# A planned single-core kernel that mixes a recurrent attention with a full attention: new ranks for its list scheduler, smaller filler pieces, and a new way to issue the start-up loads

## The chip, the cores and the metric

The kernel runs on one core of one Trainium2 chip. The metric is device time in microseconds (us) of one execution, as the median of several runs. Five engines work side by side: TensorE (PE, its weight loads shown as PEld), VectorE (DVE), ScalarE (ACT), GpSimd (POOL) and SyncE (SP). Each runs its own instructions strictly in the order of the program and waits on semaphores. Loads and stores are issued from SP's and ACT's instruction streams.

## The reference, cut to what matters

Two attentions read the same input `x` (2048 rows of 576) and their outputs are mixed by a gate per row.

```python
# A: 64 segments of 32 rows, 32 heads of 128; 8 memory rows go from segment to segment
for s in range(n_seg):
    h = concat([mem, xs])                      # 40 rows
    q, k, v = h @ Wq, h @ Wk, h @ Wv           # 576 -> 32 x 128 each
    p = softmax(mask(q k^T * scale))
    o = (p v) @ Wo
    mem = o[:8]; outs.append(o[8:])            # mem feeds the next segment
# B: full attention over 2048 rows, 32 heads of 18
qkv = x @ wqkv;  b = softmax(q k^T * scale) v @ wo
return g * a + (1 - g) * b                     # g = sigmoid(sum(x * gate_w))
```

A is a chain of 64 dependent segments. B has no such order and serves as filler work beside it.

## The kernel before, in words

**The planner.** The kernel first builds some thousands of `Op` objects with `add(name, engines, duration, fn, deps, prio, mode, take, give, tail)`. `Plan.run` is a list scheduler. It simulates the engines with the written durations, a cost of 0.1 us when TensorE changes its tiling mode (`SWITCH`), a delay from one engine to the next (`DRAIN`) and, for loads and stores, a landing time (`tail`). At each step `Plan.choose` takes, among the operations that could start within 0.03 us of the first, the one of smallest `prio` (plus 0.4 if it changes TensorE's mode). Operations with `prio` under 1 can hold back a longer one. The result is only an order: the instructions are emitted in it, and on the chip each waits for its real data. A dependency that stands only in `deps` and not in the data makes no instruction wait. Buffers are counted as tokens (`plan.tokens_of`): three PSUM banks `pb`, one `sb` of four banks for B's scores, one `ob` for B's output.

**Start-up.** `x_tile` loads 16 tiles of `x` (alternately from SP and ACT), has POOL duplicate a narrow part (`xd`), transposes on TensorE into `xT`, and evacuates with DVE and ACT. ACT's stream also issues `wqkv` (`load_wb`) and then, by `load_w`, the three A weights `wv`, `wq`, `wk`: 12 DMAs and 4.7 MB each. `project_qk` and `project_v` compute B's q, k and v and store them to DRAM (tiles `stg`, `vt`), from where `load_k`, `load_v`, `load_q` fetch them by head. `last_unit` computes q, k, v of A's last 8 rows of each segment (PE tiles `pv`, stored from `vl`): 24 units for the first 16 segments before the recurrence, and 72 later as filler, in pieces of 0.57 us or 1.1 us. `opening` marks the point where B's start-up buffers are given back; `wo` (4.7 MB) is loaded then.

**Recurrence.** For segment `s`: load of the segment's 24 rows into `ht` (`ld_h`, three DMAs on SP), six projections (`project`: Q0, K0, Q1, K1, V0, V1; PE tile `pvv`), evacuation to `tm`, `turn` (PE tile `pt`), copy to `qk`, scores `psh`, exp, mask `mn`, sums `sm` (tile `pss`), reciprocal `rq`, broadcast `bc` (tile `prb`), normalising into `et`, `pso` (needs V: `put_v`, eight DMAs `v_sb<-tm` on SP), copy to `ot`, output product in 8 pieces (`out_pieces`, tile `acc`), `obf` and `bd`, and `fold` (tile `pw`), which makes the next memory and writes it into the next `ht`. Every four segments `lo0`/`lo1` do the output product of the last rows. `st_a` stores each segment's output with four DMAs.

**B as filler.** 512 visits `sb` (four score matmuls), `ex` (exp on ACT, 2048 columns) and `ob` (four value matmuls). Visit `i` may not be planned before a segment's Q0: `ahead` visits are free, the others are spread evenly over the 64 segments; `sb` has `prio` 0.

**End.** B's output product (`po`), times the gate, plus A's rows reloaded from DRAM and multiplied on POOL (`ga`).

## Time and profile before

| | us |
|---|---|
| median of 3 runs (1756.57 to 1763.96) | 1757.65 |
| the profiled execution | 1751.69 |
| its span, first to last instruction | 1749.9 |
| TensorE busy in it | 1471.1 |
| ACT busy | 1099.5 |
| DVE busy | 715.0 |
| POOL busy | 133.2 |
| mean granted TensorE clock | 0.945 of full speed |

The span leaves 1.8 us of the execution's own time around it. Busy times add up over stages that differ: start-up, the 64 segments, the end. A stage has to be read by itself.

### The profile page before, as it was taken

Reading aid. Unit: us, or ns where it says so; the run is one execution under the profiler, and the core shown is the slowest. Engines: PE = TensorE matmul, PEld = TensorE weight load, DVE = VectorE, ACT = ScalarE, POOL = GpSimd, SP = SyncE. Lnnn points to the kernel's source line nnn. Section 1 sums busy time; section 2 is a strip of 40 time slices with the busy share of each in tenths; the row PEclk is TensorE's granted clock in tenths of the full one; section 3 lists DMA queues with packets and bytes.
Section 4 is the critical chain, followed back from the end, with each engine's and each line's share of the span. In section 5 each row is a group of like instructions: output and inputs, shape, how many; then the busy total and the mean of one; then the engine's idle time right before and its main releaser. Section 6 shows DMA issues by size and latency. Waiting matters only on the chain. (4 is left out here: it accounts for less than half of the span.)

```text
span 1749.9 us, 68709 instructions
## 1 busy us (share of the span) xinstructions
PE 1471.1 (84%) x30560; PEld 844.8 (48%) x30582; DVE 715.0 (41%) x1523; ACT 1099.5 (63%) x872; POOL 133.2 (8%) x295
## 2 busy tenths in 40 slices
PE   2387788988898988889889889888989888888886
PEld 2243544555555544455555444555555444444444
DVE  2143234444344444443434443444444444434444
ACT  1024678888776666666656666665767666667672
POOL 4000000000000000000000000000000000000024
PEclk9989889999999999999999989999999898899998
DMA  7746322111221111111222111112222111111131
GB/s 259 261 126 183 58 41 54 47 29 36 59 40 33 39 48 49 39 33 33 49 44 42 34 37 39 47 35 41 38 48 59 30 30 32 40 24 33 27 118 66
DMA packets 285727, 104.21 MB, mean 60 GB/s; under 512 B 222263, under 2 KB 281911, under 8 KB 283895
## 3 DMA queue, kind: packets, MB, share of 16 engines
q1 hardware_dynamic: 281079, 82.50, 20.2%
q10 hardware_dynamic: 4352, 17.33, 2.7%
q8 instruction: 239, 3.92, 0.9%
q14 instruction: 57, 0.47, 0.1%
HBM read 52.09 MB, written 30.86 MB: 47 GB/s over the span
## 5 line engine op out<-in xcount | busy, mean ns | idle before, releaser
L680 ACT ACTIVATE etb<-sb 128x2048 bf16<-128x2048 f32 x512 | 961.4, 1878 | 432.0 <-PE sb L671 400.2
L333 DVE CAST tm<-pvv 128x512 bf16<-128x512 f32 x312 | 214.9, 689 | 235.8 <-PE pvv L980 198.1
L980 PEld LDWEIGHTS <-ht 128*32 128x32 bf16 x7680 | 199.2, 97 | 203.7 <-issue 21.4
L671 PE MATMUL sb<-qch,kch 32*128 32x512 bf16 x2048 | 210.0, 398 | 57.1 <-ACT etb L680 55.9
L689 PE MATMUL ob<-etb,vch 128*32 128x512 bf16 x2048 | 213.4, 407 | 7.2 <-ACT etb L680 7.2
L908 PE MATMUL acc<-wo,ot 128*32 128x144 bf16 x8192 | 182.5, 253 | 10.0 <-DVE ot L333 8.1
L908 PEld LDWEIGHTS <-ot 128*32 128x32 bf16 x8192 | 165.0, 111 | 29.8 <-DVE ot L333 15.8
L980 PE MATMUL pvv<-wq_m,ht 128*32 128x512 bf16 x2048 | 138.6, 388 | 14.5 <-DVE ht L1175 13.8
L671 PEld LDWEIGHTS <-kch 32*128 32x128 bf16 x2048 | 62.8, 91 | 179.0 <-issue 157.1
L1047 DVE COPY qk<-pt 128x1024 bf16<-128x1024 bf16 x128 | 88.1, 688 | 143.3 <-PE pt L1039 142.6
L333 DVE CAST ot<-pso 128x320 bf16<-128x320 f32 x176 | 82.7, 484 | 142.6 <-PE pso L1124 141.3
L980 PE MATMUL pvv<-wk_m,ht 128*32 128x512 bf16 x2048 | 137.4, 385 | 0.0
L980 PE MATMUL pvv<-wv_m,ht 128*32 128x512 bf16 x2048 | 134.1, 379 | 0.0
L950 POOL COPY qk<-xl 128x256 bf16<-128x256 bf16 x128 | 53.2, 418 | 1051.9 <-PE psh L1060 852.4
L689 PEld LDWEIGHTS <-vch 128*32 128x32 bf16 x2048 | 55.0, 94 | 117.5 <-issue 115.3
L1124 PE MATMUL pso<-et,v_sb 64*128 64x40 bf16 x2048 | 62.8, 183 | 51.2 <-DMA v_sb<-tm 36.4
L1039 PE MATMUL pt<-ident,tm 128*128 128x128 bf16 x1024 | 78.6, 219 | 9.9 <-DVE obf L1204 5.4
L331 ACT CAST ot<-pso 128x320 bf16<-128x320 f32 x80 | 34.0, 426 | 83.4 <-PE pso L1124 82.8
L1124 PEld LDWEIGHTS <-v_sb 64*128 64x128 bf16 x2048 | 43.4, 96 | 80.9 <-DMA v_sb<-tm 47.6
L1039 PEld LDWEIGHTS <-tm 128*128 128x128 bf16 x1024 | 61.4, 97 | 42.4 <-issue 40.5
L1113 DVE TENSOR_TENSOR et<-et,prb 128x320 bf16<-128x320 bf16 x128 | 59.1, 485 | 24.0 <-PE prb L1103 21.3
L1153 DVE CAST obf<-acc 128x144 bf16<-128x144 f32 x64 | 19.7, 307 | 120.6 <-PE acc L908 88.3
(117 smaller groups left out, 1452.6 us busy)
## 6 DMA issues: line engine op xcount, KB each, us to landing
v_sb<-tm SPq DMA_DIRECT2D x512, 32.0 KB
qkd<-vl SPq DMA_DIRECT2D x64, 128.0 KB
xl<-qkd SPq DMA_DIRECT2D x64, 128.0 KB
wo<-in_A_Wo_dram SPq DMA_DIRECT2D x4, 1152.0 KB
wv_m<-in_A_Wv_dram ACTq DMA_DIRECT2D x4, 1024.0 KB
vgd<-vt SPq DMA_DIRECT2D x32, 128.0 KB
wq_m<-in_A_Wq_dram ACTq DMA_DIRECT2D x4, 1024.0 KB
wk_m<-in_A_Wk_dram ACTq DMA_DIRECT2D x4, 1024.0 KB
```

The lines of the kernel that those rows point to most:

```text
L331: nc.scalar.copy(out=out_of(), in_=in_of())
L333: nc.vector.tensor_copy(out=out_of(), in_=in_of())
L671: nc.tensor.matmul(sb[:, j, :], lhsT=kc[r, o:o + P], rhs=qt_[r, :], start=True, stop=True, tile_position=(32 * j, 0),)
L680: nc.scalar.activation(out=etb[:, :, :], in_=box["sb", gq, kb][:, :, :], func=ACT.Exp, scale=scale_b)
L689: nc.tensor.matmul(ob[32 * j:32 * j + 32, :], lhsT=vc[:, o + 32 * j:o + 32 * j + 32], rhs=etb[:, j, :], start=(kb == 0), stop=(kb == NKB - ...
L908: nc.tensor.matmul(acc[32 * j:32 * j + 32, :], lhsT=o[:, slot, t0:t0 + CT], rhs=wo[:, h, RW * j:RW * j + RW], start=(first and s_ == 0), s ...
L950: nc.gpsimd.tensor_copy(out=opened["qk"][:, f, :, 0:16 * L].rearrange("p a (h t) -> p a h t", t=L)[:, :, :, CT:L], in_=box["xlt", s][:, :, ...
L980: nc.tensor.matmul(pv[32 * j:32 * j + 32, :], lhsT=ht[:, cc, :], rhs=rw, start=(c == 0), stop=(c == NF), tile_position=(0, 32 * j), skip_g ...
L1039: nc.tensor.transpose(out=pt[:, a, :, i, :], in_=tm[:, i * Dh:(i + 1) * Dh], identity=ident[:, :])
L1047: nc.vector.tensor_copy(out=opened["qk"][:, hf, :, 0:16 * L].rearrange("p a (h t) -> p a h t", t=L)[:, :, :, 0:CT], in_=box["pt", s, hf][: ...
L1113: nc.vector.tensor_tensor(out=et[:, :], in0=et[:, :], in1=box["prb", s, hf][:, :], op=ALU.mult)
L1124: nc.tensor.matmul(ps[jj][:, r * L:(r + 1) * L], lhsT=v_sb[rr, hf * 1024 + r * Dh:hf * 1024 + (r + 1) * Dh], rhs=et[rr, r * L:(r + 1) * L] ...
```

## The change

The fixed priorities become entries of a table `RANK`, and some constants of the scheduler too (the cost of a mode switch 0.4 to 0.358, the window 0.03 to 0.016, the hold-back rules). Visits: `ahead` 60 to 23, `behind` 6 to 0. A unit of filler (`last_unit`) is cut into four or five pieces, and may be planned only after `psh0` of its segment instead of after Q0; `lo0`/`lo1` of a group are planned in the next segment, after its `psh0`. The A weights are issued by SP in 12 chunks of three DMAs, each planned after the last but one has landed; `wqkv` by SP too, `gw` later. The memsets of POOL become planned operations, `xd` goes from POOL to DVE. More buffers: `xn` 6 to 8, `stg` 4 to 6, `vt` 3 to 6, `vl` 2 to 3. The segment's rows come from one load of three DMAs per four segments (`ld_x` into `xg`) and three POOL copies per segment (`put_x`); `st_a` stores four segments with four DMAs. SP's planned time of `put_v` goes from 1.8 to 2.4 us.

```diff
+RANK = {
+    "switch": 0.358, "near": 0.016, "early": 0.142, "wait": 0.207, "Q0": 1.286, "K0": 1.258, "Q1": 1.601,
+    "K1": 1.792, "V0": 1.857, "V1": 1.908, "t0": 0.05, "t1": 0.05, "ph0": 1.897, "ph1": 1.655, "sm0": 1.072,
+    "sm1": 1.075, "bc0": 1.274, "bc1": 1.098, "po0": 0.49, "po1": 0.786, "op0": 1.401, "op1": 0.286,
+    "fo": 0.05, "lo0": 2.219, "lo1": 2.052, "la": 1.802, "ob": 1.25, "eQ": 3.281, "eK": 2.028, "eV": 1.472,
+    "co": 0.984, "le": 5.423, "xp": 0.119, "mn": 0.05, "fin": 3.122, "la_gate": 1, "lo_gate": 1, "ahead": 23,
+    "behind": 0, "tail": 0.059,
+}
...
-    for t_ in kring + qring + [wo7]:
-        nc.gpsimd.memset(t_[:], 0.0)
...
+    z_wb = zero("zwb", wb[TL:P, NF, :], 1.6, 0.05)
...
-    plan.tokens_of("xn", 6)
+    plan.tokens_of("xn", 8)
...
-    plan.tokens_of("stg", 4)
-    plan.tokens_of("vt", 3)
+    plan.tokens_of("stg", 6)
...
-        du = add(f"xd{n}", "POOL", 0.35, dup, [ld], prio=0.1, take=("xd",))
+        du = add(f"xd{n}", "DVE", 0.2, dup, [ld], prio=0.1, take=("xd",))
...
-    def load_wb(e):
+    def load_wb(c):
+        def fn(e):
+            dma(out=wb[:, c, :], in_=rows(B_wqkv, c))
+            dma(out=wb[TR * c:TR * c + TR, NF, :], in_=B_wqkv[RW * c + P:RW * c + RW, :])
+
+        return add(f"wb{c}", "SP", 0.8, fn, [z_wb], prio=0.14, tail=load_time(442) + 1.0)
+
+    wbl = [load_wb(c) for c in range(NF)]
+    weight_loads = {}
+    chain = [wbl[-2], wbl[-1]]
+    for w, src, name in ((wv, A_Wv, "wv"), (wq, A_Wq, "wq"), (wk, A_Wk, "wk")):
+        w2 = src.rearrange("d h e -> d (h e)")
         for c in range(NF):
-            nc.scalar.dma_start(out=wb[:, c, :], in_=rows(B_wqkv, c))
-            nc.scalar.dma_start(out=wb[TR * c:TR * c + TR, NF, :], in_=B_wqkv[RW * c + P:RW * c + RW, :])
+            def load_w(e, w=w, w2=w2, c=c):
+                dma(out=w[0][:, c, :], in_=rows(w2, c))
+                for two in range(2):
...
+            chain.append(add(f"{name}{c}", "SP", 1.2, load_w, [chain[-2]], prio=0.7, tail=6.8))
+        weight_loads[name] = chain[-4:]
...
-        if kind == 2:
-            a0 = a = add(f"la{tag}", "PE", 5 * 0.216, mm_v, deps, prio=prio, mode="full", take=("pb",))
-        else:
-            a0 = add(f"la{tag}", "PE", 10 * 0.057, mm_qk(0), deps, prio=prio, mode="full", take=("pb",))
-            a = add(f"lb{tag}", "PE", 10 * 0.057, mm_qk(2), [a0], prio=prio - 0.01, mode="full")
+        parts, a = [], None
+        for k in range(NF + 1 if kind == 2 else NF):
+            a = add(
+                f"la{tag}.{k}", "PE", 0.216 if kind == 2 else 5 * 0.057, part(k), [a] if a else deps,
...
-        lh = add(f"lh{s}", "SP", 1.2, ld_h, [opening, xstores[s * seg // QC], prev2.get("V1")], prio=0.7, tail=2.5)
+        if s % 4 == 0:
+            def ld_x(e, s=s):
...
+        def put_x(e, s=s, ht_i=ht_i):
+            ht, xg, t = opened["ht", ht_i], box["xg", s // 4], slice(s % 4 * seg, s % 4 * seg + seg - LO)
+            nc.gpsimd.tensor_copy(out=ht[:, 0:NF, M:CT], in_=xg[:, 0:NF, t])
...
-        pv0 = add(f"qv0.{s}", "SP", 1.8, put_v(0), [ev0, prev.get("pso0")], prio=0.2, give=(("tm", ev0, 0),), tail=1.9)
+        pv0 = add(f"qv0.{s}", "SP", 2.4, put_v(0), [ev0, prev.get("pso0")], prio=0.2, give=(("tm", ev0, 0),), tail=1.9)
...
+        if s % 4 == 3:
+            def st_a(e, s=s):
...
-                last_unit(q, kind, b, 1.8, uq0)
+                last_unit(q, kind, b, RANK["la"], gates_of[RANK["la_gate"]])
...
-    ahead, behind = 60, 6
+    ahead, behind = RANK["ahead"], RANK["behind"]
```

## Rows read from the trace of the kernel before

**Rows 1.** Windows: stretch, length, busy PE PEld DVE ACT POOL, clock, DMA share, GB/s.
```profile
0.00:31.00 31.00, 12.89 (x79) 8.93 (x81) 8.76 (x31) 5.75 (x22) 19.05 (x66) 1.00 0.78 247
31.00:70.00 39.00, 0.00 (x0) 0.00 (x0) 0.26 (x1) 0.00 (x0) 0.69 (x3) 1.00 0.90 332
...
166.00:178.70 12.70, 1.46 (x16) 0.58 (x16) 0.73 (x2) 3.88 (x3) 0.00 (x0) 0.67 0.95 292
178.70:224.50 45.80, 35.06 (x449) 24.71 (x449) 13.39 (x24) 32.79 (x19) 0.00 (x0) 0.90 0.36 50
...
254.80:1688.00 1433.20, 1263.28 (x28271) 724.08 (x28285) 613.24 (x1317) 979.85 (x768) 77.09 (x187) 0.95 0.18 39
...
1716.00:1750.00 34.00, 22.83 (x286) 16.45 (x286) 15.89 (x33) 5.84 (x4) 10.14 (x7) 0.90 0.19 64
```

**Rows 2.** Waits of TensorE, 0 to 224.5: total us, times, longest.
```profile
PE ptx L384 <- ACT xL L403: 44.5, 3, 39.8
...
PE ptm L873 <- DVE vl L333: 9.4, 1, 9.4
PE ptx L385 <- POOL xd L376: 7.0, 1, 7.0
```

**Rows 3.** Waits of ACT, same stretch.
```profile
ACT xL L403 <- DMA wk_t<-in_A_Wk_dram: 46.9, 1, 46.9
```

**Rows 4.** Timeline of ACT's stream at start-up: start, us, what.
```profile
23.25 9.38 ACTq L447 DMA_DIRECT2D wv_m<-in_A_Wv_dram  x4
...
70.36 0.18 ACT L403 COPY xL<-ptx 64x32 bf16<-64x32 bf16 x1 [46.86 <-DMA wk_t<-in_A_Wk_dram]
```

**Rows 5.** DMA traffic, 31 to 70.
```profile
DMA packets 3923, 12.95 MB, mean 332 GB/s; under 512 B 1554, under 2 KB 2297, under 8 KB 2634
```

**Rows 6.** Timeline of SP's stream before the first segment.
```profile
188.51 23.24 SPq L808 DMA_DIRECT2D qkd<-vl  x11
```

**Rows 7.** Instruction groups by shape, 0 to 224.5: busy, mean ns, idle before.
```profile
L680 ACT ACTIVATE etb<-sb 128x2048 bf16<-128x2048 f32 x33 | 62.0, 1877 | 56.2 <-PE sb L671 30.0 <-PE ob L689 26.1
```

**Rows 8.** One line, the write of the new memory: first and last start.
```profile
L1175 DVE CAST ht<-pw x63: 170/208/208, 254.8 to 1688.0; 128x48 bf16<-128x48 f32 x63
```

**Rows 9.** Waits of TensorE, 254.8 to 1688.
```profile
PE pso L1124 <- DMA v_sb<-tm: 33.4, 52, 2.1
PE sb L671 <- ACT etb L680: 33.1, 77, 1.4
PE pw L1167 <- DVE bd L1156: 17.4, 35, 0.9
PE prb L1103 <- DVE rq L1095: 15.1, 35, 0.6
PE pvv L980 <- DVE ht L1175: 13.5, 42, 0.8
PE acc L908 <- DVE ot L333: 8.1, 16, 0.6
...
PE pso L1124 <- DVE ot L333: 7.1, 11, 0.7
PE pso L1124 <- DVE et L1113: 6.6, 16, 0.8
```

**Rows 10.** Timeline of SP in the second segment.
```profile
264.63 0.39 SPq L936 DMA_DIRECT2D ht<-xtd  x1
...
266.32 5.43 SPq L1019 DMA_DIRECT2D v_sb<-tm  x8
```

**Rows 11.** Timeline of TensorE around one visit.
```profile
888.13 0.39 PE L980 MATMUL pvv<-wk_m,ht 128*32 128x512 bf16 x4
888.45 0.40 PE L671 MATMUL sb<-qch,kch 32*128 32x512 bf16 x4
...
889.00 0.82 PE L980 MATMUL pvv<-wk_m,ht 128*32 128x512 bf16 x12
889.65 0.39 PE L980 MATMUL pvv<-wk_t,ht 128*32 128x512 bf16 x4
```

More of the change, by code (lines that the diff above doesn't have):

```diff
@@ L151, in choose @@
         first = min(f[0] for f in found)
-        near = [f for f in found if f[0] <= first + 0.03]
+        near = [f for f in found if f[0] <= first + RANK["near"]]
         def rank(f):
             op = f[1]
-            switch = 0.0 if e != "PE" or op.mode == mode else 0.4
+            switch = 0.0 if e != "PE" or op.mode == mode else RANK["switch"]
             return (op.prio + switch, op.seq)
@@ L369, in load @@
             eng.dma_start(out=xn[:], in_=x_td[n * P:(n + 1) * P, :])
-        ld = add(f"x{n}", "SP" if n % 2 == 0 else "ACT", 0.4, load, prio=0.1, take=("xn",), tail=load_time(147) + 0.25 * n)
+        ld = add(
+            f"x{n}", "SP" if n % 2 == 0 else "ACT", 0.42, load, prio=0.1, take=("xn",), tail=load_time(147) + 0.2 * n
+        )
         def dup(e):
@@ L542, in mm @@
                 )
-        a = add(f"pv{hf}{kb}", "PE", 5 * 0.122, mm, [wbl, *xdone[kb][:2]], prio=prio, mode="full", take=("pb",))
+        a = add(f"pv{hf}{kb}", "PE", 5 * 0.122, mm, [*wbl, *xdone[kb][:2]], prio=prio, mode="full", take=("pb",))
         k = hf * NKB + kb
-        vt = vts[k % 3]
+        vt = vts[k % 6]
         def ev(e):
@@ L552, in ev @@
             )(e)
-        before = v_stores.get((k - 3) if k >= 3 else None)
+        before = v_stores.get((k - 6) if k >= 6 else None)
         b = add(
-            f"ve{hf}{kb}", ("DVE", "ACT"), (psum_copy(288), act_time(288)), ev, [a, before], prio=1.5, give=(("pb", a, 0),)
+            f"ve{hf}{kb}", ("DVE", "ACT"), (psum_copy(288), act_time(288)), ev, [a, before, z_vt[k % 6]], prio=1.5, give=(("pb", a, 0),)
         )
@@ L757, in last_unit, with part @@
         j, hf = divmod(b, 2)
-        def mm_v(e):
-            box["pl", q, kind, b] = pv = bank([P, 512], FP32, "pv")
-            for c in range(NF + 1):
-                rw, cc = w_slice(wv, c, b * 512, 512)
-                nc.tensor.matmul(pv[:, :], lhsT=xL[:, cc, cols], rhs=rw, start=(c == 0), stop=(c == NF))
-        def mm_qk(lo):
+        def part(k):
             def fn(e):
-                w = wq if kind == 0 else wk
-                if lo == 0:
+                if k == 0:
                     box["pl", q, kind, b] = bank([P, 512], FP32, "pv")
@@ L797, in ev @@
                 )(e)
-        ev_ = add(f"le{tag}", ("DVE", "ACT"), (psum_copy(512), act_time(512)), ev, [a], prio=3.0, take=("vl",), give=(("pb", a0, 0),))
+        ev_ = add(f"le{tag}", ("DVE", "ACT"), (psum_copy(512), act_time(512)), ev, [a], prio=RANK["le"], take=("vl",), give=(("pb", a0, 0),))
         def st(e):
@@ L1064, in psh @@
                         )
-            p_ = add(f"ph{hf}.{s}", "PE", 0.41, psh, [c_, pl], prio=1.20 + 0.01 * hf, mode="half", take=("pb",))
+            p_ = add(f"ph{hf}.{s}", "PE", 0.41, psh, [c_, pl], prio=RANK[f"ph{hf}"], mode="half", take=("pb",))
             cur[f"psh{hf}"] = p_
@@ L1088, in sm @@
                     )
-            s_ = add(f"sm{hf}.{s}", "PE", 0.1, sm, [m_], prio=1.18 + 0.01 * hf, mode="full", take=("pb",))
+            s_ = add(f"sm{hf}.{s}", "PE", 0.1, sm, [m_], prio=RANK[f"sm{hf}"], mode="full", take=("pb",))
             def rc(e, hf=hf, s=s):
@@ L1107, in bc @@
                         )
-            b_ = add(f"bc{hf}.{s}", "PE", 0.2, bc, [r_], prio=1.16 + 0.01 * hf, mode="half", take=("pb",))
+            b_ = add(f"bc{hf}.{s}", "PE", 0.2, bc, [r_], prio=RANK[f"bc{hf}"], mode="half", take=("pb",))
             def nm(e, hf=hf, s=s):
@@ L1159, in ob_bd @@
             )
[L1161 removed]
+        c1 = add(f"oc{s}", "DVE", psum_copy(144), ob_cast, [mids[1]], prio=0.3, take=("obf",) if s % 4 == 0 else ())
+        if s % 4 == 0:
+            c1_first, folds = c1, []
         c2 = add(f"bd{s}", "DVE", psum_copy(64), ob_bd, [mids[1], c1, prev.get("fold")], prio=0.3, give=(("pb", acc_state["op0"], 0),))
@@ L1169, in fold @@
                 nc.tensor.matmul(pw_[:, NF + 1, :], lhsT=bd[:, 0:2 * TL], rhs=sel[:, :], start=True, stop=True)
-            fo = add(f"fo{s}", "PE", 0.1, fold, [c1, c2], prio=1.0, mode="full", take=("pb",))
+            fo = add(f"fo{s}", "PE", 0.1, fold, [c1, c2], prio=RANK["fo"], mode="full", take=("pb",))
             cur["fold"] = fo
@@ L1211, in lo_store @@
                     dma(out=dst[:, :, RW * j:RW * j + RW], in_=box["lbf", s][32 * j:32 * j + 32, :])
-            so = add(f"so{s}", "SP", 1.5, lo_store, [lc_], prio=2.0, give=(("obf", lc_, 0),), tail=2.5)
+            so = add(f"so{s}", "SP", 2.4, lo_store, [lc_], prio=2.0, give=(("lbf", lc_, 0),), tail=2.5)
             for k in range(4):
                 a_stores[s - k].append(so)
+        if i4 == 3:
+            lo_deps = [hist[s - k]["otl"] for k in range(4)]
+            pend_lo.append((s, gi, lo_deps))
+        gates_of = [uq0, cur["psh0"], cur["psh1"], cur["pso0"], cur["out0"], cur["pso1"]]
+        if pend_lo and (pend_lo[0][0] < s or s == n_seg - 1):
+            last_out(*pend_lo.pop(), None if s == n_seg - 1 else gates_of[RANK["lo_gate"]])
         if s < 48:
```

192 lines of the change are left out of this document (98 added, 94 removed).

## Prediction

> **What bounds the kernel now.** I read the windows first, cutting the span where the work changes [rows 1]. Three stages stand out. Start-up lasts to 224.5 us, where the first projection of segment 0 begins. The recurrence runs from there to 1716. The end takes the last 34 us.
>
> Start-up holds the clearest fault. From 31 to 70 us TensorE is busy 0.00 us of 39, ACT 0.00 and DVE 0.26, while the DMA share is 0.90. TensorE waits there for an evacuation by ACT (39.8 us at the longest) [rows 2], and ACT's own wait of 46.9 us ends with the last piece of `wk` [rows 3]. The timeline says why: from 23.25 to 70.36 ACT's stream issues the A weights and nothing else [rows 4]. No arithmetic waits for those weights then. It waits for the engine that issues them, because that stream is held until the DMA engines take the work: 12.95 MB go by in this time at 332 GB/s [rows 5].
>
> A second start-up stall lies at 166 to 178.7: TensorE busy 1.46 of 12.70 us, DMA share 0.95 [rows 1]. There 9.4 us of wait go to the `vl` buffer [rows 2]. SP has issued the 4.7 MB of `wo`, and stores behind them wait. From 178.7 to 224.5 the work is split between filler units, visits and the `qkd` stores, eleven of which hold SP for 23.24 us [rows 6].
>
> In the recurrence the new memory is written 63 times, first at 254.8 and last at 1688.0 [rows 8]: 1433.2 / 62 = 23.1 us per segment. TensorE is busy 1263.3 of these 1433.2 us (88%), ACT 68%, DVE 43%, POOL 5% [rows 1]. So TensorE's order is what counts. Its 169.9 us of idle time are made of many short waits: 33.4 us for V's way through DMA, 33.1 us for ACT to free the scores, and links of the segment's own chain: 17.4, 15.1, 13.5, 8.1, 7.1 and 6.6 us, together 67.8 [rows 9]. The granted clock is 0.95 of full [rows 1], so about 5% of 1433.2, some 72 us, goes to stretches at the lower of the two levels (1.2 instead of 2.4 GHz).
>
> **The change part by part: start-up.** Moving the weights from ACT to SP takes 36 issues out of ACT's stream, so the evacuations of 31 to 70 us run at once. The 14.2 MB still have to come in, about 43 us at 332 GB/s, now beside the projections, whose stores and reloads share the DMA engines and stand in SP's order behind weight chunks. The spacing stands in the plan alone: no instruction waits for the chunk before last. The bounds: if nothing else holds TensorE, the whole 39 us come back; if SP's stream stalls as it did behind `wo` (1.46 of 12.70 us busy [rows 1]), only 12% of 39, 5 us. I take the middle with a lean to the better end, since the chunks have stores planned between them and `stg` and `vt` hold twice or 1.5 times as many tiles: TensorE about 60% busy, 24 us.
>
> Zeroing when needed: `xd` waits 7.0 us for POOL's memsets [rows 2]. It goes to DVE, which is busy 8.76 of the first 31 us [rows 1]. But `wqkv` has to land before any projection, so of the 7 us I count 5; bounds 0 and 7. The 8 `wqkv` issues go to SP; that costs nothing while x and `wqkv` fill the DMA engines anyway (share 0.78 in 0 to 31).
>
> Fewer visits ahead: 33 exps lie before 224.5 [rows 7]. With `ahead` at 23, ten move into the recurrence. One visit costs TensorE 889.00 - 888.13 - 0.22 = 0.65 us, the 0.22 being the projection group ahead of it, as (889.65 - 889.00) / 3 shows [rows 11]. In 178.7 to 224.5 ACT is busy 32.79 us with visits beside 35.06 us of TensorE [rows 1]; without most of its 19 ACT instructions TensorE has about 35.06 - 12 = 23 us of work, and the `qkd` stores at 23.24 / 11 = 2.1 us each make 16 x 2.1 = 34 us of SP. So that stretch goes from 45.8 to about 34: 12 us. Bounds: 0 (the stores stretch with the traffic) and 20. The `wo` stall stays; a third `vl` tile takes perhaps 1 us off it. Start-up in all: 24 + 5 + 12 + 1 = 42 us, between 5 and 67.
>
> **The recurrence.** Per segment SP loses three `ht` issues out of four times (264.63 to 266.32, 1.7 us [rows 10]), which stood right ahead of V's eight issues, and the four stores out of four times likewise. The planner now also counts 2.4 us per half for V, and the eight take 5.43 us [rows 10], nearer than 2 x 1.8. I take half of the 33.4 us: 17. Bounds 0 and 33.
>
> Small pieces held back until after `psh0`: they can fill waits of 0.2 to 0.9 us, which pieces of 0.57 and 1.1 us cannot do without delaying the chain. They exist in 48 of 64 segments. Of the 67.8 us I take a third, 23; bounds 0 and two thirds, 45. The 33.1 us for ACT's scores stay. The clock's share follows the idle time: (17 + 23) / 169.9 x 72 = 17 us; bounds 0 and 33. Against this stand ten visits at 0.65 us, 6.5, and more mode changes: 72 units go from 120 pieces (24 x 1 + 48 x 2) to 312, and if a quarter of the 192 new ones stand alone, two changes of 0.10 us each (888.45 - 888.13 - 0.22 [rows 11]) make 48 x 0.2 = 10 us; bounds 0 and 38. Recurrence: 17 + 23 + 17 - 6.5 - 10 = 40.5 us, between -45 and +105.
>
> `put_x` costs POOL three copies per segment. By POOL's mean of 77.09 / 187 = 0.41 us [rows 1] that is 64 x 1.2 = 79 us on an engine idle for 1356 us; it can run as soon as V1 two segments back is done, so a whole segment covers it. If POOL stood in a wait for `psh` at that time, the next Q0 would be late by up to 1.2 us. I take nothing, and keep 0 to 20 us for the range (a quarter of the segments late by 1.2). Grouped stores, `gw` later and the reordered evacuations cost nothing that TensorE waits for: SP and DVE have 50% and more free.
>
> **The end.** By the shares (512 - 23) / 64 = 7.6 against (512 - 66) / 64 = 7.0 the last segment is left with 512 - 23 - 63 x 7.64, some 8 visits, where it had 13. The end is 34 us with TensorE busy 22.83 [rows 1]. I take 4 us off; bounds 0 and 11.
>
> **Sum.** 42 + 40.5 + 4 = 86.5 us. The profiled execution took 1751.69 us (span 1749.9), so 1665; the median of the runs shown lies 6.0 us above that execution, and so the forecast is 1671.
>
> **The rivals.** *The stall moves to SP.* Weights, stores and reloads now stand in one stream; TensorE waits for `stg`, `vt` and `qch` instead of for ACT, and the start-up gives only the lower bound, 5 us, while the plan's new order brings nothing in the recurrence but its visits and mode changes (-16.5) and the end 4: 1757.65 + 7.5 = 1765 at the worst, or, with half of each gain, 1715. For it speaks the stretch 166 to 178.7; against it that stores are planned between the chunks. The Trainium skill speaks for this rival too ("DMA: Bandwidth & Descriptors", "Issuing engines are not separate DMA queues"): all issuers share the same 16 DMA engines, and issuing elsewhere saves only sequencer time. The trace agrees that the transfer itself is no shorter (share 0.90) but shows 46.9 us of sequencer time that an engine needed for arithmetic lost [rows 3]; by the rule alone the weights part would bring about nothing, and the sum would be 24 us less, 1695.
>
> *The recurrence gives far more.* If two thirds of V's and the chain's waits go and the clock follows: 22 + 45 + 28 - 6.5 - 5 = 84 us, and start-up 55: 1757.65 - 84 - 55 - 6 = 1613. For it speaks that TensorE's busy 1263 us holds slow-clock time that fewer waits would shorten; against it that ranks found on planned durations do not know these waits.
>
> *The new order is worse on the chip.* The plan prices V's path, POOL and the clock only roughly. `psh0` now ranks 1.897, behind every projection but V1, so the exp of half 0 starts later and the chain to `fold` grows. If a segment lasts 1.0 us longer, 64 us go and the start-up's 42 do not pay: 1757.65 + 64 - 46 = 1776. It decides from (42 + 4) / 64 = 0.72 us per segment on.
>
> **Chances.** Forecast 0.60 (1640 to 1705), little gain 0.15 (1705 to 1765), far more 0.17 (1580 to 1640), worse order 0.08. The range that leaves out no more than 2 in 10 takes the forecast and most of the second and third: 1600 to 1735. No change can be told from about 0.5%, 9 us here. Faster than 1749: 0.60 + 0.17 + 0.12 = 0.89; within: 0.03 from the second case and 0.01 from the worse order, 0.04; slower: 0.07.
>
> **What would show it.** Right for start-up: no stretch of 39 us without TensorE between 20 and 75 us, ACT evacuating there, the first projection of segment 0 near 183 us. Wrong: waits of TensorE on `stg` or `vt` evacuations released by stores, SP's stream full from 20 to 80 us. Right for the recurrence: 62 intervals of the memory's write near 22.5 us, TensorE's wait for `v_sb<-tm` near 17 us, a clock above 0.95, shorter waits of `pw` and `prb`. Wrong: an interval above 23.8, or new waits of `psh` and Q0 on POOL. Wrong in sum: a start-up that gains less than 20 us, or a recurrence that loses what it gained.

## The result, and the profile after

The changed kernel takes 1576.07 us (median of 4 runs, 1574.38 to 1580.68) against 1760.08 us for the kernel before in the same comparison: a ratio of 0.896, interval 0.893 to 0.899. The profiled execution took 1575.17 us, its span is 1573.5 us, its mean granted clock 0.963. The forecast was 1671 us, between 1600 and 1735. The direction was right and the gain more than twice as large, 184 us against 86.5. The profiled execution of the kernel before (1751.69 us) lies 8.4 us under its median here, so the two spans differ by 176.4 us only.

Windows of the changed kernel, with the columns of [rows 1]:

```profile
0.00:31.00 31.00, 15.45 (x110) 10.43 (x111) 14.44 (x51) 8.40 (x34) 18.57 (x67) 0.94 0.89 287
31.00:70.00 39.00, 25.72 (x137) 12.64 (x137) 9.83 (x20) 10.19 (x7) 0.00 (x0) 0.70 0.70 211
...
202.80:1522.90 1320.10, 1236.49 (x28473) 697.75 (x28473) 653.67 (x1373) 996.52 (x740) 114.24 (x370) 0.98 0.19 43
1522.90:1573.50 50.60, 42.43 (x702) 29.04 (x702) 28.46 (x58) 17.01 (x11) 29.55 (x21) 0.93 0.47 149
```

The write of the new memory, one line with its first and last start:

```profile
L1205 DVE CAST ht<-pw x63: 168/207/209, 202.8 to 1522.9; 128x48 bf16<-128x48 f32 x63
```

With this line and [rows 8] these 176.4 us split into four parts. The first projection of segment 0 starts at 179.7 instead of 224.7: 45 us. From there to the first write of the memory it takes 23.1 us instead of 30.1: 7 us. The 62 intervals between writes take 1320.1 instead of 1433.2 us (21.29 each instead of 23.12): 113.1 us. What follows the last write takes 50.6 instead of 61.9 us: 11.3 us. The forecast had 42, nothing, 40.5 and 4. So the start-up came out as forecast in its sum, and the recurrence is where the forecast fell short.

**Start-up.** Waits of TensorE, 0 to 170 us, for [rows 2]:

```profile
PE pq L517 <- DVE stg L340: 17.1, 6, 6.6
PE ptm L887 <- DVE vl L340: 10.3, 1, 10.3
PE pvb L554 <- DVE vt L340: 10.1, 3, 4.0
...
PE ptx L403 <- DVE xd L394: 1.3, 1, 1.3
```

The 44.5 us behind ACT's `xL` are gone (3.6 remain), and TensorE works 25.72 of the 39 us in which it did nothing. But 27.2 us of waits for `stg` and `vt` have come in their place: evacuations that wait for a free tile, so for a store (DVE itself waits 24.2 us for stores of `vt` and 20.1 us for stores of `stg` in this time). SP's stream shows what those stores stand behind (start, us, what):

```profile
38.07 4.55 SPq L539 DMA_DIRECT2D ktd<-stg  x4
...
52.06 0.42 SPq L458 DMA_DIRECT2D wq_m<-in_A_Wq_dram  x1
...
54.95 7.67 SPq L575 DMA_DIRECT2D vgd<-vt  x6
...
69.86 6.22 SPq L575 DMA_DIRECT2D vgd<-vt  x5
```

One issue of a weight piece takes 0.4 us, while six stores of `vt` between them hold SP for 7.67 us. The stall has moved to SP in part, as one rival said, but it is shorter there. The wait behind `wo` (`ptm`, 9.4 before) stayed, as forecast.

**Recurrence.** Waits of TensorE from 202.8 to 1522.9, for [rows 9]:

```profile
PE pvv L1006 <- DVE ht L1205: 18.2, 51, 0.8
PE sb L686 <- ACT etb L695: 14.6, 51, 0.5
PE pso L1150 <- DMA v_sb<-tm: 14.0, 24, 2.0
PE pso L1150 <- DVE ot L340: 12.7, 26, 1.0
PE acc L924 <- issue: 9.3, 12, 2.1
...
PE pw L1197 <- DVE bd L1184: 0.9, 3, 0.3
```

TensorE's idle time in the 62 intervals fell from 169.9 to 83.6 us (1320.1 - 1236.49). V's way through DMA went from 33.4 to 14.0 and `pw` from 17.4 to 0.9. The wait for ACT's scores, which the forecast left alone, went from 33.1 to 14.6. Two links grew: the wait of the next segment's first projection for the new memory (`pvv` on `ht`) from 13.5 to 18.2, and `pso` on `ot` from 7.1 to 12.7. No wait for POOL stands among these rows, so `put_x` held nothing up. Busy time fell too, by 26.8 us, although 481 visits instead of 457 lie in these intervals, and the clock rose from 0.95 to 0.98. One segment on TensorE (start, us, what, idle before):

```profile
860.67 0.39 PE L1006 MATMUL pvv<-wk_t,ht 128*32 128x512 bf16 x4
...
863.05 0.62 PE L1065 MATMUL pt<-ident,tm 128*128 128x128 bf16 x8
...
867.18 0.62 PE L1065 MATMUL pt<-ident,tm 128*128 128x128 bf16 x8
...
868.28 1.04 PE L1006 MATMUL pvv<-wv_m,ht 128*32 128x512 bf16 x16
...
869.47 0.69 PE L1086 MATMUL psh<-qk 128*64 128x40 bf16 x32
...
870.83 0.39 PE L781 MATMUL pv<-wv_m,xL 128*128 128x512 bf16 x1
871.05 0.22 PE L1112 MATMUL pss<-bsel,et 128*128 128x2 bf16 x3
871.13 0.38 PE L781 MATMUL pv<-wv_m,xL 128*128 128x512 bf16 x1
...
871.74 0.53 PE L1129 MATMUL prb<-ident,rq 128*64 128x128 bf16 x12
```

The reader is to see three things. The transposes `pt` slip in among the projections as soon as their operand is there. The scores `psh` of both halves run in one go, after V. The filler `pv` stands in the gaps of the softmax, between `psh`, `pss` and `prb`, where TensorE waited before (`prb` on `rq`: 15.1 us before, 0.5 now).

### The profile page after: what moved, and what is told of

Read it like the earlier page. It is cut to its first block, busy times and chain, and to the rows that moved or that the text cites. A ratio compares the mean times of both kernels' runs of the same rounds, so it can differ in the third digit from the quotient of the medians.

```text
span 1573.5 us, 68449 instructions
## 1 busy us (share of the span) xinstructions
PE 1422.0 (90%) x30582; PEld 810.5 (52%) x30582; DVE 760.1 (48%) x1596; ACT 1068.3 (68%) x815; POOL 168.6 (11%) x477
## 4 chain that ended last, share of the span: by engine, by line
PE 73%; ACT 9%; DMA 7%; SPq 4%; issue 4%; DVE 3%; POOL 1%; ACTq 0%; DVEq 0%
PE pvv L1006 24%; PE sb L686 11%; PE acc L924 11%; PE ob L704 8%; ACT etb L695 8%; PE pt L1065 4%; PE pv L785 4%; DMA v_sb<-tm 3%; PE pv L781 2%; PE pso L1150 2%; SPq L1045 2%; PE pq L517 2%; PE psh L1086 1%; PE po L1340 1%; PE prb L1129 1%
## 5 line engine op out<-in xcount | busy, mean ns | idle before, releaser
L340 DVE CAST tm<-pvv 128x512 bf16<-128x512 f32 x354 | 244.4, 691 | 298.1 <-PE pvv L1006 282.1
L704 PE MATMUL ob<-etb,vch 128*32 128x512 bf16 x2048 | 209.0, 397 | 1.7 <-issue 0.8
L924 PE MATMUL acc<-wo,ot 128*32 128x144 bf16 x8192 | 160.2, 239 | 8.6 <-issue 8.5
L1006 PE MATMUL pvv<-wk_m,ht 128*32 128x512 bf16 x2048 | 142.4, 380 | 19.4 <-DVE ht L1205 18.5
L924 PEld LDWEIGHTS <-ot 128*32 128x32 bf16 x8192 | 150.5, 104 | 18.1 <-issue 13.0
L1006 PE MATMUL pvv<-wq_m,ht 128*32 128x512 bf16 x2048 | 145.1, 380 | 0.0
L340 DVE CAST ot<-pso 128x320 bf16<-128x320 f32 x195 | 89.3, 486 | 68.3 <-PE pso L1150 67.4
L961 POOL COPY ht<-xg 128x96 bf16<-128x96 bf16 x64 | 17.1, 268 | 910.9 <-PE pvv L1006 878.4
L1150 PE MATMUL pso<-et,v_sb 64*128 64x40 bf16 x2048 | 56.1, 180 | 28.0 <-DMA v_sb<-tm 14.0
L1225 POOL COPY otl<-ot 128x256 bf16<-128x256 bf16 x64 | 25.6, 399 | 327.0 <-ACT ot L338 164.5
```

Source lines behind the costliest of these rows:

```text
L340: nc.vector.tensor_copy(out=out_of(), in_=in_of())
L704: nc.tensor.matmul(ob[32 * j:32 * j + 32, :], lhsT=vc[:, o + 32 * j:o + 32 * j + 32], rhs=etb[:, j, :], start=(kb == 0), stop=(kb == NKB - ...
L924: nc.tensor.matmul(acc[32 * j:32 * j + 32, :], lhsT=o[:, slot, t0:t0 + CT], rhs=wo[:, h, RW * j:RW * j + RW], start=(first and s_ == 0), s ...
L1006: nc.tensor.matmul(pv[32 * j:32 * j + 32, :], lhsT=ht[:, cc, :], rhs=rw, start=(c == 0), stop=(c == NF), tile_position=(0, 32 * j), skip_g ...
L1150: nc.tensor.matmul(ps[jj][:, r * L:(r + 1) * L], lhsT=v_sb[rr, hf * 1024 + r * Dh:hf * 1024 + (r + 1) * Dh], rhs=et[rr, r * L:(r + 1) * L] ...
```

## The experiments

The kernel before had medians of 1753.54 to 1764.11 us beside these runs; ratios are to those. "Interval" is (last minus first write of the memory) / 62 in the profiled run, "idle" those 62 intervals less TensorE's busy time in them, "first" the start of the first projection of segment 0, "clock" the granted one in the 62 intervals. Executions of the one kernel before spread over 24 us beside these runs (1747.77 to 1771.35), and intervals come from a single execution each, so differences of 0.1 to 0.2 us per segment are not read as effects.

| run | us | ratio, interval of it | first | interval | idle | clock |
|---|---|---|---|---|---|---|
| before | 1760.08 | 1 | 224.7 | 23.12 | 169.9 | 0.95 |
| after | 1576.07 | 0.896 (0.893 to 0.899) | 179.7 | 21.29 | 83.6 | 0.98 |
| e1 | 1725.75 | 0.977 (0.973 to 0.981) | 179.2 | 23.46 | 177.2 | 0.95 |
| e2 | 1673.6 | 0.950 (0.946 to 0.953) | 180.3 | 22.65 | 146.0 | 0.97 |
| e3 | 1675.21 | 0.950 (0.947 to 0.952) | 181.7 | 22.87 | 120.6 | 0.93 |
| e4 | 1593.26 | 0.903 (0.900 to 0.906) | 180.2 | 21.61 | 85.8 | 0.96 |
| e5 | 1583.16 | 0.903 (0.898 to 0.907) | 178.1 | 21.27 | 85.3 | 0.98 |
| e6 | 1677.37 | 0.957 (0.952 to 0.962) | 177.7 | 22.91 | 127.4 | 0.94 |
| e7 | 1709.5 | 0.975 (0.971 to 0.979) | 179.8 | 23.29 | 149.9 | 0.96 |
| e8 | 1687.04 | 0.964 (0.958 to 0.969) | 178.3 | 22.97 | 147.5 | 0.95 |
| e9 | 1591.05 | 0.905 (0.901 to 0.909) | 190.4 | 21.28 | 83.1 | 0.98 |
| e10 | 1667.04 | 0.949 (0.945 to 0.952) | 179.3 | 22.67 | 139.4 | 0.95 |
| e11 | 1698.8 | 0.967 (0.963 to 0.971) | 181.2 | 23.16 | 159.3 | 0.98 |
| e12 | 1575.69 | 0.897 (0.893 to 0.901) | 180.0 | 21.30 | 76.8 | 0.97 |
| e13 | 1758.06 | 1.000 (0.997 to 1.002) | 216.3 | 23.27 | 170.7 | 0.94 |
| e14 | 1583.72 | 0.900 (0.897 to 0.903) | 198.6 | 21.21 | 82.9 | 0.98 |
| e15 | 1615.38 | 0.919 (0.915 to 0.922) | 163.8 | 21.68 | 101.9 | 0.98 |
| e16 | 1594.4 | 0.905 (0.901 to 0.909) | 162.7 | 21.42 | 87.4 | 0.98 |
| e17 | 1606.76 | 0.913 (0.909 to 0.916) | 180.0 | 21.25 | 82.1 | 0.97 |

### Four parts of the change, done or undone

**e1**: the new kernel with all ranks, `ahead` and `behind`, the filler's pieces and gates, the loads of the segment's rows and SP's planned time of `put_v` as before; only the start-up is new. 

> The changed start-up alone (weights and wqkv from SP in chunks, zeroing as planned operations, xd on DVE, more start-up buffers) with the segments as in the kernel before: old ranks and scheduler constants, old filler pieces and gates, ahead 60 and behind 6, loads and stores once per segment. Theory S (start-up is worth what the trace of after shows, about 45 us, and the segments 113 us apart from it): near 1760 - 45 = 1715, interval of the memory write still 23.1 us. Rival (the segments are faster because V's path and the queues got freer from a better start): below 1680, interval below 22.6.

**e2**: the new kernel with the old ranks and scheduler constants; 23 visits ahead, pieces, gates and loads stay new. Two of the seven lines:

```diff
-    "switch": 0.358, "near": 0.016, "early": 0.142, "wait": 0.207, "Q0": 1.286, "K0": 1.258, "Q1": 1.601,
-    "K1": 1.792, "V0": 1.857, "V1": 1.908, "t0": 0.05, "t1": 0.05, "ph0": 1.897, "ph1": 1.655, "sm0": 1.072,
+    "switch": 0.4, "near": 0.03, "early": 0.15, "wait": 0.12, "Q0": 1.4, "K0": 1.41, "Q1": 1.42,
+    "K1": 1.43, "V0": 1.44, "V1": 1.45, "t0": 1.3, "t1": 1.3, "ph0": 1.2, "ph1": 1.21, "sm0": 1.18,
...
```

> The changed kernel with the 33 priorities and four scheduler constants of before; pieces, gates, visits, loads and start-up stay changed. Theory R (the order of the segment's own operations brings most of the 113 us): 1650 to 1700, interval 22.5 to 23.2 us. Rival F (small pieces held back fill the waits whatever the ranks are): under 1620, interval under 21.9.

**e3**: the new kernel with the old filler, whole pieces and old gates, and the new ranks. Its edit is that of e5 and e6 together, below. 

> The changed kernel with the fillers of before: units in pieces of 0.57 and 1.1 us, planned after Q0 of their segment, the last rows' product in its own segment; ranks stay changed. Theory F: 1640 to 1690. Theory R: under 1610, since the order is kept. Both: 1610 to 1640.

**e4**: the new kernel with three loads and four stores per segment again. Two lines of the edit:

```diff
...
-        lh = add(f"lh{s}", "POOL", 0.75, put_x, [lx, prev2.get("V1")], prio=0.7, give=(("xg", lx, 0),) if s % 4 == 3 else ())
+        lh = add(f"lh{s}", "SP", 1.2, ld_h, [opening, xstores[s * seg // QC], prev2.get("V1")], prio=0.7, tail=2.5)
...
```

> The changed kernel with the segment's rows loaded by three DMAs each segment and stored by four each segment, no copies on POOL. Theory R and F: within 10 us of 1576. Rival Q (SP's stream was what delayed V, and the freed 3 us per segment bring the gain): 1610 or more, TensorE's wait for v_sb back near 33 us.

The result lies between the two expectations. The start-up alone brings 45.5 us at its own place and leaves the interval at 23.46. Beside e1, the new gates and loads without ranks (e2) bring 23.46 - 22.65 = 0.81 us per segment, the ranks and loads without the gates (e3) 0.59. All together bring 2.17. So 0.77 us per segment, 48 us in 62 intervals, come only from having ranks and gates at once, and more if the loads, which both sums hold, are counted once. The grouped loads (e4) are worth 0.32 us per segment; V's wait is 21.6 us there, against 14.0 in the new kernel and 13.3 with the new loads and the old ranks (e2). The planned 2.4 us for V was not undone by itself.

### Gate, size, and the order of the links

**e5** puts back the whole pieces (0.57 and 1.1 us) with the new gates, **e6** the old gates with the small pieces. The edit of e6:

```diff
...
-        if pend_lo and (pend_lo[0][0] < s or s == n_seg - 1):
-            last_out(*pend_lo.pop(), None if s == n_seg - 1 else gates_of[RANK["lo_gate"]])
+        if pend_lo:
+            last_out(*pend_lo.pop(), None)
...
-    "co": 0.984, "le": 5.423, "xp": 0.119, "mn": 0.05, "fin": 3.122, "la_gate": 1, "lo_gate": 1, "ahead": 23,
+    "co": 0.984, "le": 5.423, "xp": 0.119, "mn": 0.05, "fin": 3.122, "la_gate": 0, "lo_gate": 1, "ahead": 23,
...
```

> The changed kernel with filler units in the old two sizes (1.1 us for v, 0.57 us for q and k) but with the new gates. If the size of the pieces fills the waits: 1630 to 1670, TensorE idle in the segments back above 110 us. Rival (the gate does it, that is, when the units may run): within 25 us of 1576.

> The changed kernel with small pieces but the old gates: units from Q0 of their segment, the last rows' product in its own segment. If the gate does it: 1640 to 1680, near the run with both undone. Rival (size): under 1610.

The size is worth nothing per segment (21.27); that e5's time is still some 7 us longer lies ahead of the intervals, as its memory is first written at 211.1 instead of 202.8. Of the two, the gate carries all: without it the interval is 22.91 and the clock 0.94. TensorE of e6 in one segment:

```profile
859.05 0.39 PE L785 MATMUL pv<-xL,wq_m 128*128 128x128 bf16 x4
...
861.97 0.69 PE L1086 MATMUL psh<-qk 128*64 128x40 bf16 x32
...
867.55 0.43 PE L924 MATMUL acc<-wo,ot 128*32 128x144 bf16 x16 [1.05 <-DVE ot L340]
...
869.69 0.27 PE L1150 MATMUL pso<-et,v_sb 64*128 64x40 bf16 x7 [1.07 <-DMA v_sb<-tm]
```

Filler starts among the projections, where nothing waits, and is used up when `ot` and V are late: 1.05 and 1.07 us of nothing. The windows of e6 by groups of segments (0 to 15, 15 to 31, 31 to 47, 47 to 62; same columns) agree with it:

```profile
201.73:545.66 343.93, 314.86 (x6983) 179.79 (x6980) 163.78 (x342) 249.44 (x180) 26.62 (x90) 0.96 0.19 43
...
917.28:1293.05 375.77, 342.00 (x7448) 196.96 (x7448) 171.62 (x360) 257.18 (x192) 29.03 (x97) 0.93 0.19 43
1293.05:1622.19 329.14, 300.43 (x6643) 169.14 (x6639) 151.45 (x322) 233.22 (x170) 27.45 (x87) 0.91 0.12 31
```

and those of the new kernel beside them:

```profile
202.83:521.56 318.73, 302.98 (x6942) 170.80 (x6942) 162.54 (x337) 250.75 (x185) 27.40 (x90) 0.99 0.21 46
...
858.61:1197.24 338.63, 318.09 (x7433) 179.56 (x7434) 169.62 (x356) 257.70 (x195) 29.69 (x97) 1.00 0.22 48
1197.24:1522.91 325.67, 296.90 (x6667) 166.45 (x6666) 154.18 (x326) 232.24 (x167) 27.47 (x87) 0.93 0.12 31
```

In the last group, which has no units of `last_unit`, the two agree (329.14 and 325.67 us for 15 intervals). In the first they differ by 25.2 us.

**e7** sets the turns' ranks back in the new kernel; **e8** is e1 with the reverse of that edit and nothing else; **e11** sets the scores' ranks back.

```diff
...
-    "K1": 1.792, "V0": 1.857, "V1": 1.908, "t0": 0.05, "t1": 0.05, "ph0": 1.897, "ph1": 1.655, "sm0": 1.072,
+    "K1": 1.792, "V0": 1.857, "V1": 1.908, "t0": 1.3, "t1": 1.3, "ph0": 1.897, "ph1": 1.655, "sm0": 1.072,
...
-    "K1": 1.792, "V0": 1.857, "V1": 1.908, "t0": 0.05, "t1": 0.05, "ph0": 1.897, "ph1": 1.655, "sm0": 1.072,
+    "K1": 1.792, "V0": 1.857, "V1": 1.908, "t0": 0.05, "t1": 0.05, "ph0": 1.2, "ph1": 1.21, "sm0": 1.072,
...
```

The first pair of lines is e7's, the second e11's.

> The changed kernel with only the two ranks of the transposes of q and k back at 1.30 (they were 0.05, ahead of nearly all else). If these two carry the order's gain (the transposes run between the projections, so that the scores, the softmax and V's transfer overlap with the other projections): 1660 or more. Rival (the gain is spread over many ranks): under 1620.

> The changed start-up, old segments, old fillers and ranks, but the two ranks of the transposes at 0.05. If these two alone carry it: 1726 falls to 1650 to 1690. Rival (they work only with late scores and held-back fillers): 1700 or more.

> The new kernel with the scores psh0 and psh1 back at ranks 1.20 and 1.21, ahead of every projection not yet begun. Theory (late scores keep the halves together and leave filler, which waits for psh0, as the only thing to do while the softmax runs): with early scores V is pushed behind them, intervals of 21.8 to 23 us, time 1605 to 1680 us. Rival of the prediction (late scores lengthen the chain from the exponential to the fold): intervals below 21.0 us and a time below 1560.

Undoing two numbers of the table costs almost the whole gain of the recurrence (e7: 23.29, e11: 23.16), while adding the turns' two to the old order brings only 0.49 us per segment (e8, whose time came out inside the range for the turns alone, at its slow end). e11 is slower than its own theory allowed. One segment of TensorE in e7:

```profile
867.87 0.43 PE L1086 MATMUL psh<-qk 128*64 128x40 bf16 x16
868.24 0.40 PE L785 MATMUL pv<-xL,wq_m 128*128 128x128 bf16 x4
...
869.73 0.39 PE L1006 MATMUL pvv<-wv_m,ht 128*32 128x512 bf16 x4
...
872.71 0.43 PE L1086 MATMUL psh<-qk 128*64 128x40 bf16 x16
```

Here the first half's scores come before V's second half is projected. That opens the gate of the filler, whose rank 1.802 goes ahead of V1's 1.908. V1 runs from 869.73 on between pieces of filler, and the second half's scores follow 4.8 us after the first. In the new kernel both halves' scores are one group of 32 matmuls. The transposes themselves stand where they stood (863.18 and 867.32 here, 863.05 and 867.18 above), so how their rank leads to this order was not traced. In e11 the halves' scores are apart too (853.36 and 857.50 us in one segment), and V and ACT's scores are waited for again, as these waits of TensorE in its 62 intervals show:

```profile
PE sb L686 <- ACT etb L695: 44.2, 82, 1.4
PE pso L1150 <- DMA v_sb<-tm: 39.7, 61, 2.0
```

**e10** was meant as the smallest sufficient set. 

> The kernel before with the start-up changes, grouped loads, and of the recurrence only four things: both turns at rank 0.05, small pieces, both gates on psh0, and the late ranks of the scores (1.897 and 1.655). All other ranks are old, and 60 visits are ahead. Theory (these carry the gain, as filler then stands in the chain's gaps): intervals of 21.2 to 22.0 us, TensorE's clock 0.97 or more, time 1590 to 1635 us. Rival (the gain needs the whole set of ranks searched together): intervals of 22.5 us or more, time above 1655.

The kernel that ran had whole pieces and ungrouped loads, unlike what that text says. By e4 and e5 that explains about 0.3 us of its 22.67; the theory missed by more, and the rival's range was met. **e15** and **e16** start from the new kernel with the old ranks (e2) and add groups of new ones. 

> The new kernel, of whose ranks only those of the two turns, the two scores and the six projections are new; softmax, broadcast, output, fold, filler, visits, evacuations and the planner's four switching numbers are at their old values; gates, small pieces, grouped loads and 23 visits ahead stay new. Theory (the order projections, scores, then filler is what the gain needs): intervals of 21.5 to 22.2 us, clock 0.97 or more, time 1590 to 1635 us. Rival (the softmax-to-fold ranks carry as much as the projections'): intervals above 22.5 us, time above 1640.

> The same, with the new ranks of softmax, broadcast, pso, output and fold as well, so that only those of the filler, the visits' values, the evacuations and the planner's switching numbers are old. Theory (all links of the segment have to be ordered together, the rest is worth little): within 20 us of the new kernel, 1576 to 1596 us, intervals 21.3 to 21.6. Rival (the fillers' and evacuations' ranks matter too): above 1610 us.

Both came out as their theories said. So turns, scores and projections bring 22.65 - 21.68 = 0.97 us per segment, the links from the softmax to the fold another 0.26, all other ranks and the scheduler's constants 0.13, which is not clear of the spread. (Segment 0 of e15 and e16 begins earlier than in the new kernel, and its memory is written later, at 214.2 and 210.9.) What e10 lacked above all, as far as its difference to e15 can be added up like this, was the projections' order: in it V (1.44, 1.45) stands behind Q and K but far ahead of every score and filler, and K0 behind Q0.

### Start-up

**e13** makes one move alone on the kernel before, **e9** undoes the same move alone in the new kernel, **e14** undoes the deeper `stg` and `vt`.

```diff
...
-            chain.append(add(f"{name}{c}", "SP", 1.2, load_w, [chain[-2]], prio=0.7, tail=6.8))
+        chain.append(add(name, "ACT", 6.0, load_w, [*wbl], prio=0.16 + 0.01 * k, tail=16.0 + 15.0 * k))
...
```

The edit of e9 stands above, that of e13 is its reverse, and this is e14's:

```diff
...
-    vts = [pw.tile([P, HB // 2, 32], BF16, name=f"vt{i}") for i in range(6)]
+    vts = [pw.tile([P, HB // 2, 32], BF16, name=f"vt{i}") for i in range(3)]
...
-    plan.tokens_of("stg", 6)
+    plan.tokens_of("stg", 4)
...
```

> The kernel before with one thing of the change: SP issues the A weights in the chain of 12 pieces, and ACT no longer does; wqkv, x, zeroing, rings, ranks, gates and 60 visits ahead stay old. The prediction's term: TensorE's 39 us without work shrink by 24, so the first projection comes near 200 us instead of 224.5 and the time falls by about 24 us (1725 to 1740). Theory after the run with ACT issuing again (undoing cost 10.7 us there): 8 to 14 us. Rival (the stall moves to SP's order and to the small stg and vt rings): the first projection at 218 us or later, less than 6 us won. A gain of 35 us or more would say that this one move is the whole start-up's gain and that the other parts only stand in for it.

> The new kernel, in which ACT again issues the 36 pieces of the A weights in three lumps (one for each of wv, wq, wk), while x, wqkv, the zeroing, the deeper stg, vt and vl rings, the order and the gates stay new. Theory (ACT's stream, held by those issues, was the start-up's stall): TensorE stands still again for some 35 to 40 us between 20 and 75 us, the first projection of segment 0 comes at 205 to 222 us instead of 179.7, the intervals of the memory write stay at 21.3, and the time is 1600 to 1618 us. Rival (deeper rings and later zeroing made the gain, not the issuing engine): the first projection stays within 6 us of 179.7 and the time below 1585.

> The new kernel with the rings of the B projections' stores as before: stg 4 tiles instead of 6, vt 3 instead of 6. Theory (with the weights in SP's order, evacuations wait for stores, and the deeper rings cover part of it): TensorE's waits on stg and vt evacuations before 170 us grow from 27 us to 40 or more, and the first projection comes 8 to 20 us later than 179.7; the intervals stay; time 1584 to 1598 us. Rival (the transfers set the pace, the rings only move the wait): the first projection within 4 us, time below 1581.

Waits of ACT and, below, of TensorE in e9:

```profile
ACT xL L421 <- DMA wk_t<-in_A_Wk_dram: 46.5, 1, 46.5
```

```profile
PE ptx L402 <- DMA wk_t<-in_A_Wk_dram: 45.9, 1, 45.9
...
PE pvb L556 <- DVE vt L340: 2.8, 2, 2.4
```

The stall of 46 us is back in full, and the first projection comes only 10.7 us later, between the two expectations. Two things take the rest back. The waits for `stg` and `vt` shrink from 27.2 to 4.0 us (2.8, and 1.2 of `pgs` on `vt`), as all A weights have landed by the time TensorE goes on: idle time before the first projection grows by 20.2 us only (76.8 against 56.6). And busy time falls by 9.5 us (113.58 against 123.08, for 977 and 981 matmuls). The same projections take longer in the new kernel (first two lines) than in e9:

```profile
L517 PE MATMUL pq<-xT,wb 128*128 128x512 bf16 x160 | 42.1, 420 | 17.1 <-DVE stg L340 17.1
L554 PE MATMUL pvb<-wb,xT 128*128 128x288 bf16 x160 | 26.3, 334 | 10.1 <-DVE vt L340 10.1
...
L519 PE MATMUL pq<-xT,wb 128*128 128x512 bf16 x160 | 36.6, 390 | 0.0
L556 PE MATMUL pvb<-wb,xT 128*128 128x288 bf16 x160 | 21.9, 300 | 2.8 <-DVE vt L340 2.8
```

The granted clock is 0.70 from 31 to 70 us in the new kernel, where TensorE works between short waits, and 0.93 from 70 to 118 us in e9, where it is busy 41.99 us of 48.

Without the deeper rings in the new kernel (e14) the first projection comes 18.9 us later, but not by the waits that the theory named: those for `stg` and `vt` are 25.7 us, no more than the 27.2 of the new kernel. Idle time before the first projection grows by 9.0 us and busy time by 9.9, with 23 exps before it instead of 14; why segment 0 starts later is open. In the whole time the rings are worth 0.900 against 0.896, with intervals that overlap.

The move alone (e13) gives 224.7 - 216.3 = 8.4 us: 15.4 us less idle time (73.0 against 88.4) and 7.0 us more busy time, with 39 exps instead of 34. Waits of TensorE in e13:

```profile
PE sb L667 <- ACT etb L676: 14.5, 13, 2.0
PE pq L498 <- DVE stg L333: 13.1, 3, 6.6
...
PE ptx L385 <- POOL xd L376: 6.6, 1, 6.6
```

The time as a whole did not change in e13 (1.000): its recurrence is 9.5 us longer than in the profile of the kernel before, which lies 8.4 us under its own median. Whether the recurrence suffered by more than the accident of another plan stays open. The small gain agrees better with the rule of the Trainium skill that the prediction weighed ("DMA: Bandwidth & Descriptors", "Issuing engines are not separate DMA queues") than with the 24 us that the prediction gave this move.

**e12**: `ahead` 60 instead of 23 in the new kernel. 

> The new kernel with 60 visits instead of 23 planned ahead of the first segment. The prediction's term (each visit ahead delays the first segment): the first projection 12 us or more later than 179.7, and the time the same or up to 10 us worse. Rival (the start-up's length is set by its transfers, so the visits ahead are free, and each takes 0.65 us out of the recurrence): the first projection within 4 us of 179.7, some 15 visits or more before it, intervals 0.2 to 0.4 us shorter, time 1550 to 1565 us. A third way: the visits do not run ahead although planned so, since their K, Q and V reloads come late, and nothing changes (1570 to 1580).

The third way came true. Fourteen exps lie before the first projection in both, and the time is the same. (In e1, which has 60 ahead too, it is also fourteen.) The planner fits in what it has room for until segment 0 can begin; the number only allows it.

### A version meant to beat both

**e17** takes visits from the full segments and gives them to the last 16.

```diff
-            s = min(int((i - ahead) / share), n_seg - 1)
+            few, many = 7.2, (NB - ahead - behind - 48 * 7.2) / (n_seg - 48)
+            k = i - ahead
+            s = int(k / few) if k < 48 * few else 48 + int((k - 48 * few) / many)
+            s = min(s, n_seg - 1)
```

> The new kernel with the visits shared out unevenly: 7.2 per segment in the first 48 segments, which also hold filler, and about 9.0 in the last 16, which hold none (7.64 in all of them in the new kernel). Theory A (the first 48 segments are full, so that each visit taken out saves its 0.65 us, 21 x 0.65 = 14 us, while the last 16 have 2 us of idle time each and a lower clock, and take 1.3 more visits at less than their cost): first three groups at 20.8 to 21.0 us, the last at 21.9 to 22.3, time 1562 to 1574. Theory B (a segment's length is set by its chain of links in a fixed order, and visits only fill what is free): first three groups stay at 21.1 and more, the last grows, time 1578 or more.

Neither theory came true as a whole. The first 31 intervals became shorter (20.96 and 20.70 against 21.25 and 21.07) with 231 exps instead of 244, so visits there do cost time; the third group did not (21.29 against 21.16). But the last group took 120 exps instead of 115, not the 20 more that were planned, and 25 instead of 9 were left to the end. The 16 more at 1.88 us of ACT are 30 us, and the end grew from 50.6 to 82.8. No version that ran is faster than the new kernel; e12 equals it.

## Why the prediction failed, point by point

**Start-up, 42 us forecast, 45 measured: the sum right, the reasons half right.** The trace splits the 45: TensorE's idle time before the first projection fell from 224.7 - 136.32 = 88.4 to 179.7 - 123.08 = 56.6 us, 31.8 us, and its busy time by 13.2. The forecast's 24 + 5 + 1 = 30 us for stalls is the first number. It gave the 24 to the move off ACT with the rings as a help. The runs show 8.4 us for the move alone and 10.7 for undoing it, while undoing the rings costs 18.9. The prediction priced new waits in place of the stall, but not that the projections themselves take longer between such waits (68.4 us in the new kernel against 58.5 in e9, for 160 matmuls each of `pq` and `pvb`). The zeroing was right: the wait for `xd` went from 7.0 to 1.3 us. The 12 us for fewer visits ahead has the right size (20 visits fewer at 0.65 us are 13) and the wrong cause: `ahead` changes nothing (e12). What took the visits out is open. It is not the stall: with it back (e9) 13 exps lie before the first projection, and without it in the old kernel (e13) 39. That the sum fits is therefore luck in part.

**The step that failed: the recurrence, 40.5 us forecast, 113.1 measured.** Every link of the sum is known now:

| term | forecast | measured |
|---|---|---|
| V's way (33.4 to 14.0) | 17 | 19.4 |
| the chain's six waits (67.8 to 32.6) | 23 | 35.2 |
| ACT's scores (33.1 to 14.6) | 0 | 18.5 |
| waits not listed | 0 | 13.2 |
| busy time: clock +17, visits -6.5, mode changes -10 | 0.5 | 26.8 |
| sum | 40.5 | 113.1 |

The 32.6 are 0.9 (`pw`), 0.5 (`prb`), 18.2 (`pvv`), 12.7 (`pso` on `ot`), 0.3 (`pso` on `et`) and nothing for `acc` on `ot`; the 13.2 are the rest of 86.3. So the mechanism was seen, filler in the chain's gaps, and mis-sized in three places. First, "of the 67.8 us I take a third, 23" was put down to pieces that are small and held back. The size brings nothing (e5); it is the gate, which is worth 22.91 - 21.29 = 1.62 us per segment with the new ranks (e6), while with the old ones gates, pieces and loads together bring 0.81 (e1, e2). The ranks themselves had no term in the sum. That they work by keeping both halves' scores together behind V is argued from single segments and from the waits of e7 and e11, not shown. Of V's 19.4 us, 7.6 come from the grouped loads (e4). Second, "the 33.1 us for ACT's scores stay" was wrong: with filler at hand TensorE has something to do while ACT works; with the old gates this wait is 34.2 us (e6). Third, busy time and the clock. The forecast took the clock's share in proportion to 40 us of idle time and charged 16.5 us against it. The table of the runs does not bear that proportion out: e11 has 159.3 us of idle time at 0.98, e6 127.4 at 0.94. Busy time fell by 26.8 us with 24 more visits inside (24 x 0.65 = 15.6 us, by the price of [rows 11]), so some 42 us of TensorE's work went, an estimate from those rows. What went is not the clock alone, as two groups show in the 62 intervals before (first of each pair) and after:

```profile
L908 PE MATMUL acc<-wo,ot 128*32 128x144 bf16 x7936 | 176.1, 253 | 10.0 <-DVE ot L333 8.1 <-issue 1.7
L924 PE MATMUL acc<-wo,ot 128*32 128x144 bf16 x7936 | 155.6, 239 | 8.6 <-issue 8.5
...
L1060 PE MATMUL psh<-qk 128*64 128x40 bf16 x1984 | 52.7, 188 | 8.2 <-DVE qk L1047 6.2 <-POOL qk L950 1.5
L1086 PE MATMUL psh<-qk 128*64 128x40 bf16 x1984 | 43.4, 187 | 0.1
```

The output product lost 20.5 us and each of its matmuls got shorter, as with a higher clock. The scores lost 9.3 us with matmuls as long as before: there it is the order: in the segments around 850 and 1100 us, two groups of 16 matmuls (0.43 us each) stood mostly apart before, and one of 32 takes 0.69 us now. How the 42 us divide was not worked out, though the rise from 0.95 to 0.98 alone would be of this size (5% of 1433.2 less 2% of 1320.1 is 45 us, an estimate). The charged 10 us for mode changes did not show up: with whole pieces (e5) the busy time is 1233.37 us instead of 1236.49.

**The rivals.** "The recurrence gives far more" named the right direction and still ended at 1613. What it held against itself, that ranks found on planned durations do not know these waits, did not hold them back: the intervals fell from 22.65 to 21.29 us by the ranks and the scheduler's constants alone (e2 against after). "The new order is worse on the chip" saw late scores as a lengthening of the chain; e11 shows that early scores cost 1.87 us per segment in this order. "The stall moves to SP" came true for 27.2 us of waits, but inside a shorter start-up.

**The end, 4 forecast, 11.3 measured.** It stays at 60.9 and 61.3 us in e7 and e2 and falls to 48.9 in e6, so the ranks, the turns' among them, bring it and not the number of visits ahead (8 or 9 exps lie in the end in all four). Which link it is was not traced.

## What to carry to other kernels

When a change reorders work and also says when filler may run, let the whole idle time of the stage with its share of the lower clock (here 169.9 us and some 72) be the upper bound, not a part of each listed wait: order and filler paid 2.17 us per segment together, against 0.81 and 0.59 each. Undoing one part of such a change measures how the part fits the others, not what it brings; the four undoings e2, e6, e7 and e11 cost 97 to 133 us each and add up to far more than the 184 us gained. A stall that is removed at the head of a stage gives back only what the next resource does not take: here 46 us of stall were worth 8.4 us at the first projection with the old rings (e13) and 10.7 with the deeper ones (e9).
